# Filling the idle half of the PE array: two chunks of F of the last step, made beside the last turns of the second row tile

## The chip, the cores and the metric

The kernel runs on one core of a Trainium2 chip. Its measure is the device time of one execution in microseconds (us). Before the change the median of 3 runs is 686.38 us (685.98 to 687.02). The profile is one more execution of the same program, 683.8 us from its first to its last instruction. PE is the matrix engine (TensorE), PEld its weight loads, DVE the vector engine, ACT the scalar engine, POOL GpSimd and SP the queue that issues most transfers.

A matmul of this program holds one operand (the stationary one) in a part of the 128 x 128 array of PE and lets the columns of the other (the moving one) stream through. The part is a tile of rows x columns, written `64*64` in the profile: rows are the partitions that the sum runs over, columns are the partitions of PSUM that receive the result. "Row tile 0" means partitions 0 to 63 of the operands, "row tile 1" partitions 64 to 127. The two can work at once.

## The reference

```python
def _attn_ref(x, weight):            # x: 8 x 4096 x 192, weight: 8 heads x 7 taps
    w = softmax(weight, axis=-1)     # (shortened)
    x_pad = zeros of 6 rows in front of each sequence, then x
    out[b, s, h, :] = sum over k of w[h, k] * x_pad[b, s + k, h, :]

def _moe_ref(x, w_in, w_out, beta):  # x: 32768 x 192, F = 2048
    h = x @ w_in
    g = h * (1.0 / (1.0 + np.exp(-beta * h)))
    return (g @ w_out).astype(np.float32)
```

A causal convolution of seven taps runs over each sequence, and its result goes through a two-layer network with F = 2048 hidden values. The second product, `g @ w_out`, is what the change touches: 2048 values of F are 16 chunks (`fc`) of 128, one chunk to a matmul.

## The kernel before

The 32768 tokens are two streams (`s` = 0 and 1) of 16384, and the program goes over both in 36 steps, most of them 512 tokens of each stream. In a step `mm1` makes `ph` from the convolved tokens, ACT makes `g` of it (128 partitions of F x 2 streams x 512 tokens for each of 16 chunks), and the second product of the step before is made beside it by `mm2_quarters`. There the first 64 partitions of a chunk go to row tile 0 and the last 64 to row tile 1, the two streams to the two column halves, and the 192 outputs are done in thirds (`A`, `B_`, `C`). Row tile 1 follows row tile 0 at a distance of `LAG` = 8 turns, so that the two never write one bank of PSUM at once; so after the loop 8 turns are left in which only row tile 1 has work.

```python
    A, B_, C = range(NM)
    LAG = 8
    turns = [[], [None] * LAG]
    for i in range(NQ, n_steps - 1):
        for r, thirds in enumerate(((A, B_, C), (C, A, B_))):
            turns[r] += [(i, m, fc) for m in thirds for fc in range(NF)]
    turns[0] += [None] * LAG
    turns = list(zip(*turns))

    def mm2_quarters(count):
        for _ in range(count):
            turn = turns.pop(0)
            for s in range(NS):
                for r in range(2):
                    if turn[r] is None:
                        continue
                    i, m, fc = turn[r]
                    # ... (the bank po_of[i, m] is taken at the first turn)
                    pin(nc.tensor.matmul(po_of[i, m][half_of(s), 0:n], w_out_s[half_of(r), fc, m:D:NM],
                                         g_at(i, fc)[half_of(r), s, 0:n], ...))
            # ... (a third that is complete goes out: take_third, a transpose on DVE)
```

The last step has no later step to be hidden beside. `last` first makes the 8 turns that are left, and then the second product of the last step, with matmuls over the whole array: for each stream four blocks of 128 tokens, for each block 16 chunks.

```python
    def last(i):
        t0, n = steps[i]
        mm2_quarters(len(turns))
        for s in range(NS):
            for b in range(n // 128):
                po = po_bank()
                for fc in range(NF):
                    pin(nc.tensor.matmul(po[:, 0:D], g_at(i, fc)[:, s, ts(b, 128)], w_out_s[:, fc, :],
                                         start=(fc == 0), stop=(fc == NF - 1)))
                o_sb = osb_pool.tile([128, 2, D], FP32, name="o_sp", bufs=4)
                take_out(o_sb[:, 0, :], po)
                pin(nc.sync.dma_start(out=os_[s, t0 + 128 * b:t0 + 128 * (b + 1), :], in_=o_sb[:, 0, :]))
```

The loop over the steps, shortened to what matters here:

```python
        for u in range(0, NF, du):
            mm1(i, us)                       # 12 matmuls 64*64, and ACT's silu after them
            # ...
            if i > NQ:
                mm2_quarters(NM)             # 3 turns
            vector_work(i, ...)              # the convolution of later steps, on DVE
    assert not work
    last(n_steps - 1)
```

[...]`psum_h` holds two tiles `ph` of two banks each, `psum_o` four banks `po`.

Of the kernel before, what the change touches and what calls it, by code (L numbers as in the profile page):

```python
# [10 lines left out]
FP32 = mybir.dt.float32  # L11
FP32R = mybir.dt.float32r
BF16 = mybir.dt.bfloat16
# [6 lines left out]
def kernel(  # L20
# [9 lines left out]
    nc = tc.nc  # L30

    B, S, D = x.shape
# [4 lines left out]
    NF = F // 128  # L37
    NK = 3
    Q = D // NK
    NS = 2  # L40
    TS = B * S // NS
    TILE = 512
# [3 lines left out]
    def pin(ins):  # L46

        return tc.keep_in_program_order(ins)
# [4 lines left out]
    consts = ctx.enter_context(tc.tile_pool(name="consts", bufs=1))  # L53
# [7 lines left out]
    psum_h = ctx.enter_context(tc.tile_pool(name="psum_h", bufs=2, space=bass.MemoryType.PSUM))  # L61
# [10 lines left out]
    n_steps = len(steps)  # L72
# [33 lines left out]
    w_out_s = consts.tile([128, NF, D], BF16, name="w_out_s")  # L106
    w_out_v = moe_w_out.rearrange("(c p) d -> p c d", p=128)

    def half_of(s):
        return slice(64 * s, 64 * s + 64)  # L110
# [59 lines left out]
    def po_bank():  # L170
        return psum_o.tile([128, TILE], FP32, name="po")
# [146 lines left out]
    def mm1_pair(i, u):  # L318

        n = steps[i][1]  # L320
        ph = psum_h.tile([128, NS, TILE], FP32, name="ph")
        fcs = (u, u + NF // 2)
        for kk in range(NK):
            for h in range(2):
                pin(nc.tensor.matmul(ph[:, h, 0:NS * n], w_in_s[half_of(h), kk, ts(fcs[h], 128)],  # L325
                                     xc_of[i][half_of(h), :, kk, :],
                                     start=(kk == 0), stop=(kk == NK - 1)))
        for h in range(2):
            pin(nc.scalar.activation(g_at(i, fcs[h])[:, :, 0:n],  # L329
                                     ph[:, h, 0:NS * n].rearrange("p (s t) -> p s t", s=NS), AF.Silu,  # L330
                                     scale=beta[:, fcs[h]:fcs[h] + 1]))
# [19 lines left out]
    def g_at(i, fc):  # L351
        return g_of[i, fc // (NF // 2)][:, fc % (NF // 2), :, :]
# [4 lines left out]
    def mm2_plan(i):  # L357


        prs = pairs_of(i)  # L360
        order = [(prs[p], ph, 8 * ph + 4 * p, 8 * ph + 4 * p + 4) for ph in range(2) for p in range(2)]
        plan = [[] for _ in range(NF)]
        for pr, ph, u0, u1 in order:
            for n in range(NF):
                plan[u0 + n * (u1 - u0) // NF].append((pr, ph, n))
        return plan

    def mm2(i, pr, phase, fc):
        if phase == 0 and fc == 0:
            po_of[i, pr] = po_banks()  # L370
        po = po_of[i, pr]
        for half in range(2):
            q = half ^ phase
            s, b = pr[q]
            r = half_of(half)
            pin(nc.tensor.matmul(po[q][:, 0:D], g_at(i, fc)[r, s, ts(b, 128)], w_out_s[r, fc, :],  # L376
                                 start=(phase == 0 and fc == 0), stop=(phase == 1 and fc == NF - 1)))
        if phase == 1 and fc == NF - 1:
            store(i, pr, po)

    def take_out(dst, po):
        pin(nc.vector.tensor_copy(dst, po[:, 0:D]))  # L382
# [20 lines left out]
    turns = [[], [None] * LAG]  # L403
# [3 lines left out]
    turns[0] += [None] * LAG  # L407
    turns = list(zip(*turns))

    def mm2_quarters(count):  # L410
        for _ in range(count):
            turn = turns.pop(0)
            for s in range(NS):
                for r in range(2):
# [3 lines that stand above are left out]
                    if (i, m) not in po_of:  # L418
                        po_of[i, m] = po_bank()
                    first = r == (m == C)  # L420
                    n = steps[i][1]
                    pin(nc.tensor.matmul(po_of[i, m][half_of(s), 0:n], w_out_s[half_of(r), fc, m:D:NM],  # L422
                                         g_at(i, fc)[half_of(r), s, 0:n],
                                         start=(first and fc == 0), stop=(not first and fc == NF - 1)))
            for r in range(2):
                if turn[r] is not None:
                    i, m, fc = turn[r]
                    if fc == NF - 1 and r != (m == C):
                        take_third(i, m)
# [4 lines left out]
    def take_third(i, m):  # L434
        nonlocal budget
        n = steps[i][1]
        if i not in osb_of:
            osb_of[i] = osb_pool.tile([128, TILE // L, L, NM], FP32, name="o_sb", bufs=2)
        pin(nc.vector.transpose(osb_of[i][:, 0:n // L, :, m],  # L439
                                po_of[i, m][:, 0:n].rearrange("p (b l) -> p b l", l=L)))  # L440
        budget -= (n + 60) / 0.96
        if m != B_:
            return
        t0, n = steps[i]
        for s in range(NS):
            dst = os_[s, t0:t0 + n, :].rearrange("(b l) (g d) -> g l b d", l=L, g=2)
            for g in range(2):
                p = 64 * s + L * g
                pin(nc.sync.dma_start(out=dst[g],
                                      in_=osb_of[i][p:p + L, 0:n // L, :, :].rearrange("p b l m -> p b (l m)")))  # L450

    def last(i):

        t0, n = steps[i]
        mm2_quarters(len(turns))
        for s in range(NS):
            for b in range(n // 128):
                po = po_bank()
                for fc in range(NF):
                    pin(nc.tensor.matmul(po[:, 0:D], g_at(i, fc)[:, s, ts(b, 128)], w_out_s[:, fc, :],  # L460
                                         start=(fc == 0), stop=(fc == NF - 1)))
                o_sb = osb_pool.tile([128, 2, D], FP32, name="o_sp", bufs=4)
                take_out(o_sb[:, 0, :], po)
                pin(nc.sync.dma_start(out=os_[s, t0 + 128 * b:t0 + 128 * (b + 1), :], in_=o_sb[:, 0, :]))
# [21 lines left out]
    def vector_work(i, ns, flush=False):  # L486


        nonlocal budget
        budget += ns  # L490
        while work and ((budget > 0 and work[0][0] <= i + 2) or (flush and work[0][0] <= i + 1)):
            budget -= work[0][1]
            work.pop(0)[2]()
        budget = min(budget, 0.0) if work else 0.0

    def new_g(i, half):
        n, kind = (TILE, "g") if i > 1 else (128, "gp")
        g_of[i, half] = g_pool.tile([128, NF // 2, NS, n], BF16, name=f"{kind}{half}")
# [58 lines left out]
    for i in range(n_steps):  # L557
        plan = mm2_plan(i - 1) if NP <= i <= NQ else [[] for _ in range(NF)]
        new_g(i, 0)
        if i < NP:  # L560
            new_g(i, 1)
        if i < NP:
            for u in range(NF // 2):
                mm1_pair(i, u)
                first_tile(i, u)
                for ph in (0, 1):
                    for j in range(i):
                        for fc in first_mm2.get((i, u, j, ph), ()):
                            mm2(j, prs_0, ph, fc)
                if i == 2:  # L570
                    vector_work(i, 1300, flush=u == NF // 2 - 1)
            continue
        du = 2 if steps[i][1] == 256 else 1
        for u in range(0, NF, du):
            us = range(u, u + du)
            if u == NF // 2:
                new_g(i, 1)
            mm1(i, us)
            for v in us:
                for t in plan[v]:  # L580
                    mm2(i - 1, *t)
                    if t[1] == 1 and t[2] == NF - 1:
                        budget -= 2 * (D + 60) / 0.96
            if i > NQ:
                mm2_quarters(NM)
            vector_work(i, 1307 * du * steps[i][1] // TILE, flush=u + du == NF)
    assert not work
    last(n_steps - 1)
# [1 line left out]
_INS = ['x', 'weight', 'moe_w_in', 'moe_w_out', 'moe_beta']  # L590
# [26 lines left out]
```

## Time and profile before

| | before |
|---|---|
| time, median of 3 runs | 686.38 us (685.98 to 687.02) |
| span of the profiled execution | 683.8 us |
| PE busy | 679.2 us, 99% |
| ACT busy | 584.0 us, 85% |
| DVE busy | 551.1 us, 81% |
| first product, line 343 | 5952 matmuls |
| second product beside it, line 422 | 5568 matmuls |
| second product of the last step, line 460 | 128 matmuls |
| granted PE clock | 1.000 |

Line numbers are those of the kernel file. A row of the timeline gives the start of the first instruction (us from the start of the span), how long the run of like instructions lasted, engine, line, operation, output and inputs, the shape, and how many were merged; in square brackets how long the engine had been idle before and what ended that. The ends of matmuls are modelled by the profiler, so their starts are the thing to read: the duration of a 64*64 matmul over 512 columns is given as 0.38 us, although the next one on the same part of the array starts earlier than that. The last microseconds, from about 667 us on, are where the change acts.

### The profile page before, as it was taken

What the parts mean: (1) busy time and instruction counts of PE and PEld (TensorE: products, weight loads), DVE (VectorE), ACT (ScalarE), POOL (GpSimd) and SP (SyncE); (2) the same over time, 40 slices, a digit from 0 to 9 for tenths busy, and PEclk for the clock granted to TensorE, in tenths of its full rate; (3) what the DMA queues carried; (4) which work ended last, traced back from release to release, by engine and by line L of the source; (5) the groups of instructions that cost most, each with busy time, mean ns of one, the idle gap of its engine ahead of it and who ended that gap; (6) DMA issues with size and microseconds to landing.
All of it is one profiled execution on the core that took longest, in us unless ns stands there. A gap on an engine that the chain in (4) does not pass through costs nothing.

```text
span 683.8 us, 27210 instructions
## 1 busy us (share of the span) xinstructions
PE 679.2 (99%) x12528; PEld 460.5 (67%) x12528; DVE 551.1 (81%) x886; ACT 584.0 (85%) x585; POOL 14.5 (2%) x26
## 2 busy tenths in 40 slices
PE   9999999999999999999999999999999999999998
PEld 7799887666666666666666666666666666666667
DVE  5999999999988888878889888889888889875112
ACT  7999999888888888888888888888888888888881
POOL 8000000000000000000000000000000000000000
PEclk9999999999999999999999999999999999999999
DMA  9652534244432344423344423344324343320223
GB/s 207 183 134 85 146 95 122 75 117 118 117 78 66 106 106 117 117 61 80 103 112 117 111 57 88 103 115 117 99 46 108 103 118 71 68 49 6 49 48 94
DMA packets 150418, 66.85 MB, mean 98 GB/s; under 512 B 113648, under 2 KB 149696, under 8 KB 150304
## 3 DMA queue, kind: packets, MB, share of 16 engines
q1 hardware_dynamic: 146992, 61.08, 35.0%
q0 software_dynamic: 3168, 3.93, 2.7%
q8 instruction: 98, 1.61, 1.0%
q14 instruction: 16, 0.13, 0.1%
q10 hardware_dynamic: 144, 0.10, 0.1%
HBM read 28.32 MB, written 25.17 MB: 78 GB/s over the span
## 4 chain that ended last, share of the span: by engine, by line
PE 98%; POOL 1%; DMA 1%; ACT 0%; issue 0%; DVE 0%; POOLq 0%
PE ph L343 47%; PE po L422 43%; PE po L376 4%; PE po L460 2%; PE ph L325 1%; DMA w_in_s<-in_moe_w_in_dram 1%; POOL w_in_s L113 0%; PE po L229 0%; ACT gp L329 0%; POOL xb L131 0%; PE po L215 0%; POOL sel L146 0%; DVE o_sp L382 0%; POOL ident L148 0%; POOLq L146 0%
## 5 line engine op out<-in xcount | busy, mean ns | idle before, releaser
L348 ACT ACTIVATE g<-ph,beta 128x1024 bf16<-128x1024 f32 (+2 forms) x528 | 557.3, 1063 | 80.9 <-PE ph L343 61.8
L343 PE MATMUL ph<-xc,w_in_s 64*64 64x512 bf16 (+3 forms) x5952 | 613.1, 368 | 0.0
L422 PE MATMUL po<-g,w_out_s 64*64 64x512 bf16 (+1 forms) x5568 | 580.7, 372 | 0.0
L343 PEld LDWEIGHTS <-w_in_s 64*64 64x64 bf16 (+1 forms) x5952 | 275.3, 104 | 125.3 <-issue 0.4
L422 PEld LDWEIGHTS <-w_out_s 64*64 64x64 bf16 x5568 | 290.3, 118 | 83.9
L303 DVE SCALAR_TENSOR_TENSOR acc<-xt,tapn,acc 128x512 f32<-128x512 bf16 (+2 forms) x450 | 311.1, 758 | 0.9
L439 DVE STREAM_TRANSPOSE o_sb<-po 128x512 f32<-128x512 f32 (+1 forms) x87 | 76.5, 879 | 111.5 <-PE po L422 111.5
L303 DVE SCALAR_TENSOR_TENSOR xc<-xt,tapn,acc 128x512 bf16<-128x512 bf16 (+2 forms) x90 | 63.9, 759 | 0.2
L87 DVE CAST xb<-xf 128x768 bf16<-128x768 f32 (+1 forms) x62 | 49.0, 830 | 0.2 <-DMA xf<-in_x_dram 0.2
L301 DVE TENSOR_SCALAR acc<-xt,tapn 128x512 f32<-128x512 bf16 (+2 forms) x90 | 41.0, 486 | 1.1
L376 PE MATMUL po<-w_out_s,g 64*128 64x192 bf16 x512 | 28.3, 243 | 0.0
L376 PEld LDWEIGHTS <-g 64*128 64x128 bf16 x512 | 23.5, 94 | 1.6
L382 DVE COPY o_sp<-po 128x192 f32<-128x192 f32 x28 | 9.0, 353 | 8.2 <-PE po L460 7.3
L325 PE MATMUL ph<-xcp,w_in_s 64*128 64x256 bf16 (+1 forms) x144 | 15.1, 306 | 0.5 <-DMA w_in_s<-in_moe_w_in_dram 0.2
L329 ACT ACTIVATE gp<-ph,beta 128x256 bf16<-128x256 f32 x32 | 12.7, 477 | 1.3 <-PE ph L325 1.0
L460 PEld LDWEIGHTS <-g 128*128 128x128 bf16 x128 | 10.5, 98 | 0.4 <-issue 0.4
L460 PE MATMUL po<-w_out_s,g 128*128 128x192 bf16 x128 | 10.7, 246 | 0.0
L329 ACT ACTIVATE g<-ph,beta 128x512 bf16<-128x512 f32 x16 | 9.6, 693 | 0.1
L325 PEld LDWEIGHTS <-w_in_s 64*128 64x128 bf16 x144 | 6.8, 94 | 4.1 <-issue 1.3
L376 PE MATMUL po<-w_out_s,gp 64*128 64x192 bf16 x128 | 7.6, 243 | 0.0
L376 PEld LDWEIGHTS <-gp 64*128 64x128 bf16 x128 | 6.0, 94 | 1.6
L229 PE MATMUL po<-xr,diag 64*128 64x384 f32 x49 | 7.0, 361 | 0.0
(52 smaller groups left out, 57.0 us busy)
## 6 DMA issues: line engine op xcount, KB each, us to landing
xf<-in_x_dram SPq DMA_DIRECT2D x60, 384.0 KB, 4.2
out_dram<-o_sb SPq DMA_DIRECT2D x108, 192.0 KB, 4.6
xt<-xb SPq DMA_TRANSPOSE x122, 3.1
out_dram<-o_sp SPq DMA_DIRECT2D x10, 192.0 KB, 4.0
w_out_f<-in_moe_w_out_dram POOLq DMA_DIRECT2D x4, 384.0 KB, 6.3
out_dram<-o_sb SPq DMA_DIRECT2D x8, 144.0 KB, 3.9
w_in_s<-w_in_s POOLq DMA_DIRECT2D x4, 192.0 KB, 7.4
out_dram<-o_sp SPq DMA_DIRECT2D x8, 96.0 KB, 1.8
```

The source lines that it names most:

```text
L87: pin((eng or nc.vector).tensor_copy(xbf_of[j][:, b0:b1, :, s, :].rearrange("p b k q -> p k b q"), xf_of[j][:, b0:b1, s, :].rearrange("p b ...
L301: pin(nc.vector.tensor_scalar_mul(a, src, w))
L303: pin(nc.vector.scalar_tensor_tensor(out=xc_of[i][:, k0:k1, o:o + m] if k == K - 1 else a, in0=src, scalar=w, in1=a, op0=ALU.mult, op1=ALU ...
L325: pin(nc.tensor.matmul(ph[:, h, 0:NS * n], w_in_s[half_of(h), kk, ts(fcs[h], 128)], xc_of[i][half_of(h), :, kk, :], start=(kk == 0), stop= ...
L329: pin(nc.scalar.activation(g_at(i, fcs[h])[:, :, 0:n], ph[:, h, 0:NS * n].rearrange("p (s t) -> p s t", s=NS), AF.Silu, scale=beta[:, fcs[ ...
L343: pin(nc.tensor.matmul(ph[m0:m1, s, n * e:n * e + n], w_in_s[half_of(s), kk, 128 * fc + m0:128 * fc + m1], xc_of[i][half_of(s), kk, 0:n], ...
L348: pin(nc.scalar.activation(g_at(i, fc)[:, :, 0:n], ph[:, :, n * e:n * e + n], AF.Silu, scale=beta[:, fc:fc + 1]))
L376: pin(nc.tensor.matmul(po[q][:, 0:D], g_at(i, fc)[r, s, ts(b, 128)], w_out_s[r, fc, :], start=(phase == 0 and fc == 0), stop=(phase == 1 a ...
L382: pin(nc.vector.tensor_copy(dst, po[:, 0:D]))
L422: pin(nc.tensor.matmul(po_of[i, m][half_of(s), 0:n], w_out_s[half_of(r), fc, m:D:NM], g_at(i, fc)[half_of(r), s, 0:n], start=(first and fc ...
L439: pin(nc.vector.transpose(osb_of[i][:, 0:n // L, :, m], po_of[i, m][:, 0:n].rearrange("p (b l) -> p b l", l=L)))
L460: pin(nc.tensor.matmul(po[:, 0:D], g_at(i, fc)[:, s, ts(b, 128)], w_out_s[:, fc, :], start=(fc == 0), stop=(fc == NF - 1)))
```

## The change

Beside the 8 turns in which row tile 0 has nothing to do, it is to make two chunks (`NX` = 2) of F for the four blocks of stream 0 of the last step. Row tile 0 sees only partitions 0 to 63. The lower half of a chunk lies there already; the upper half of `g` and of `w_out_s` is copied there by DVE in the last step (`copy_low`), into `g_x` and `w_x`. So each of four blocks gets four matmuls of 64 rows instead of two of 128 rows: 16 matmuls `64*128` over 192 columns, two to a turn. Four banks must be open at once for that; two are `po` banks and two come from one more `ph` tile. Afterwards the four blocks of stream 0 have only chunks 2 to 15 left.

```diff
-    def mm2_quarters(count):
-        for _ in range(count):
+    def mm2_quarters(count, beside=()):
+
+        per = -(-len(beside) // count)
+        for n_turn in range(count):
             turn = turns.pop(0)
             for s in range(NS):
                 for r in range(2):
 ... (the matmuls of the turn)
+            for mm in beside[per * n_turn:per * n_turn + per]:
+                mm()
             for r in range(2):
                 if turn[r] is not None:
                     i, m, fc = turn[r]
 ...
+    NX = 2
+    g_x = consts.tile([64, NX, TILE], BF16, name="g_x")
+    w_x = consts.tile([64, NX, D], BF16, name="w_x")
+
+    def copy_low(i):
+        pin(nc.vector.tensor_copy(w_x, w_out_s[half_of(1), 0:NX, :]))
+        for fc in range(NX):
+            pin(nc.vector.tensor_copy(g_x[:, fc, :], g_at(i, fc)[half_of(1), 0, :]))
+
     def last(i):
 
         t0, n = steps[i]
-        mm2_quarters(len(turns))
+        ph = psum_h.tile([128, NS, TILE], FP32, name="ph")
+        banks = [po_bank(), ph[:, 0, :], ph[:, 1, :], po_bank()]
+        r0 = half_of(0)
+        beside = []
+        for b in range(n // 128):
+            for fc in range(NX):
+                for g, w in ((g_at(i, fc)[r0, 0, :], w_out_s[r0, fc, :]), (g_x[:, fc, :], w_x[:, fc, :])):
+                    beside.append(lambda b=b, g=g, w=w, start=len(beside) % (2 * NX) == 0: pin(
+                        nc.tensor.matmul(banks[b][:, 0:D], g[:, ts(b, 128)], w, start=start, stop=False)))
+        mm2_quarters(len(turns), beside)
         for s in range(NS):
             for b in range(n // 128):
-                po = po_bank()
-                for fc in range(NF):
+                po = po_bank() if s else banks[b]
+                f0 = 0 if s else NX
+                for fc in range(f0, NF):
                     pin(nc.tensor.matmul(po[:, 0:D], g_at(i, fc)[:, s, ts(b, 128)], w_out_s[:, fc, :],
                                          start=(fc == 0), stop=(fc == NF - 1)))
 ...
             vector_work(i, 1307 * du * steps[i][1] // TILE, flush=u + du == NF)
+            if (i, u) == (n_steps - 1, NX + 1):
+                copy_low(i)
```

## The prediction

> **What bounds the kernel now.** I read the page first: its row of busy times and the chain that ended last.
>
> ```profile
> PE 679.2 (99%) x12528; PEld 460.5 (67%) x12528; DVE 551.1 (81%) x886; ACT 584.0 (85%) x585; POOL 14.5 (2%) x26
> ...
> PE 98%; POOL 1%; DMA 1%; ACT 0%; issue 0%; DVE 0%; POOLq 0%
> ```
>
> PE is busy throughout and carries 98% of the chain. So whatever takes time off PE's sequence at the end takes it off the total, and whatever adds to it adds to the total. DVE and ACT have slack. The change touches nothing before the last step, so I then took the timeline of the last microseconds, PE alone:
>
> ```profile
> 667.05 0.38 PE L343 MATMUL ph<-xc,w_in_s 64*64 64x512 bf16 x2
> 667.23 0.38 PE L422 MATMUL po<-g,w_out_s 64*64 64x512 bf16 x2
> 667.27 0.38 PE L343 MATMUL ph<-xc,w_in_s 64*64 64x512 bf16 x2
> 667.45 0.38 PE L422 MATMUL po<-g,w_out_s 64*64 64x512 bf16 x2
> 667.48 0.38 PE L343 MATMUL ph<-xc,w_in_s 64*64 64x512 bf16 x2
> 667.66 2.11 PE L422 MATMUL po<-g,w_out_s 64*64 64x512 bf16 x24
> 669.71 0.42 PE L460 MATMUL po<-w_out_s,g 128*128 128x192 bf16 x3
> ```
>
> Two things are to be seen. One line's pairs repeat every 0.216 us (667.05, 667.27, 667.48): that is a turn of 512 columns. And pairs of line 422 start between those of line 343, 0.03 us ahead of them, although the program puts all of line 343 of an `mm1` first: the two row tiles are at different places of the program, and row tile 1 is ahead. The sixth row says by how much. From 667.66 its 24 matmuls start over 2.11 - 0.38 = 1.73 us, that is 8 steps of 0.216, so 9 turns. Were row tile 0 working in all of them there would be 36; 24 is 3 turns with 4 matmuls and 6 with 2. The program has 8 turns with row tile 1 alone, so two of them were already done beside row tile 0's last work. What row tile 0 has free is about 6 x 0.216 = 1.30 us less the 0.03 us, 1.26 us.
>
> The same stretch on the vector engine:
>
> ```profile
> 668.56 0.89 DVE L439 STREAM_TRANSPOSE o_sb<-po 128x512 f32<-128x512 f32 x1 [2.12 <-PE po L422]
> 669.81 0.87 DVE L439 STREAM_TRANSPOSE o_sb<-po 128x512 f32<-128x512 f32 x1 [0.36 <-PE po L422]
> 671.24 0.36 DVE L382 COPY o_sp<-po 128x192 f32<-128x192 f32 x1 [0.56 <-PE po L460]
> 672.56 0.36 DVE L382 COPY o_sp<-po 128x192 f32<-128x192 f32 x1 [0.96 <-PE po L460]
> 673.88 0.36 DVE L382 COPY o_sp<-po 128x192 f32<-128x192 f32 x1 [0.96 <-PE po L460]
> ```
>
> The transposes at 668.56 and 669.81 are the last thirds of row tile 0 and of row tile 1, 1.25 us apart, which agrees with 1.26. A block of 16 full-array matmuls is ready every 1.32 us, so one costs 82.5 ns.
>
> Last I looked at every place where PE goes from one tile shape to another, with narrow windows of the timeline. The first two rows are the end of the 64*64 work, the next two the one place where 64*128 gives way to 64*64 (the step in which `mm1` changes its shape), the last two a change from 128*128 to 64*128.
>
> ```profile
> 669.17 0.60 PE L422 MATMUL po<-g,w_out_s 64*64 64x512 bf16 x4
> 669.70 0.20 PEld L460 LDWEIGHTS <-g 128*128 128x128 bf16 x3 [0.40 <-issue]
> ...
> 74.70 0.49 PE L376 MATMUL po<-w_out_s,g 64*128 64x192 bf16 x7
> 75.12 0.14 PEld L343 LDWEIGHTS <-w_in_s 64*64 64x64 bf16 x8 [0.16 <-issue]
> ...
> 19.53 0.39 PE L215 MATMUL po<-ident_b,xb 128*128 128x128 bf16 x4
> 19.84 0.10 PEld L376 LDWEIGHTS <-gp 64*128 64x128 bf16 x2
> ```
>
> The last start of a row is its start plus its length less one duration. First pair: 669.17 + 0.60 - 0.376 = 669.39; the next matmul starts at 669.71 with its weight load: 0.31 us instead of 0.216, so 0.09 lost. Second: 74.70 + 0.49 - 0.243 = 74.95, next at 75.12: 0.17 instead of 0.0825, again 0.09. Third: 19.53 + 0.39 - 0.219 = 19.70, next at 19.84: 0.145 instead of 0.057, 0.09. So three changes of shape cost 90 ns each, whatever the shapes, and the next weight load never starts earlier, while inside one shape it is hidden.
>
> [...]
>
> **The change part by part.**
>
> Removed: two of 16 chunks for four blocks, 8 full-array matmuls x 82.5 ns = 0.66 us off PE's sequence.
>
> Added on DVE: three copies over 64 partitions, two of 512 and one of 384 elements. A copy of 128 x 384 elements out of PSUM took 0.36 us (the copy at 19.78 us of the timeline), so about 1.2 us at most as an estimate from it. DVE sat idle for 13.14 us before the transpose at 665.55 us, and the copies are issued early in the last step, over 10 us ahead of their use. Cost 0.
>
> The banks: the new `ph` tile must wait for the silu of the last `mm1` but one. ACT ran that from 666.63 to 667.74 us; the first use of the tile is in the third of the eight turns, later than that. The `po` banks belonged to thirds that were taken out long before. Cost 0.
>
> Added on PE: 16 matmuls 64*128 over 192 columns. Were they only work on an idle row tile, 16 x 82.5 ns = 1.32 us against the 1.26 us that are free: hidden but for 0.06 us. But the program puts two of them behind the 64*64 pair of each turn. Each turn so changes the mode twice, and a mode change stops both row tiles, not only the one that changes. That also ends row tile 1's lead. Step by step, with the starts of before:
> - Turn 1 of the eight: its pair can still run ahead (667.88, one turn after the 667.66 of before). The first added matmul must wait for row tile 0's last one to end: that starts in the third turn of that row, at 668.13 with the 0.03 us, plus 0.216 plus 0.09 = 668.44.
> - Its two matmuls: 94 ns for the first (after the change at 669.71 the second matmul starts 94 ns later, because the load is not hidden) and 82.5 for the second, then 0.09 for the change back: the pair of turn 2 starts at 668.71.
> - Each further turn: pair 0.216, plus about 0.025 for its load (after 75.12 the next turn of 384 columns comes 0.187 us later instead of 0.162), plus 0.09, plus 0.094, plus 0.0825, plus 0.09: 0.60 us instead of 0.216.
> - The pair of turn 8 starts at 668.71 + 6 x 0.60 = 672.31, its first added matmul at 672.64, the second at 672.74, and the first full-array matmul at 672.74 + 0.0825 + 0.09 = 672.91, where before it started at 669.71: 3.20 us later.
>
> Sum: +3.20 - 0.66 = +2.54 us, and 686.38 + 2.54 = 688.9 us. Nothing behind it changes: blocks come every 1.16 us in stream 0 and every 1.32 in stream 1, DVE needs 0.36 for each, and the last copy and its transfer (3.3 us from 680.48 to 683.8) stay as they are.
>
> **The rivals.**
> - The added matmuls are hidden, as meant: two shapes on different row tiles run at once. Then -0.66 + 0.06 = -0.60 us, 685.8 us. For it: the row tiles do run apart from each other. Against it: row tile 1 never ran on across a change of shape in this trace, and the kernel itself gives `mm1` 64*128 in the steps whose second product is 64*128, and 64*64 only where that is 64*64.
> - Only one direction of the change drains, or the drain is shorter where the streaming work is short: about half of 3.2, +1.0 us, 687.4 us. Against it: 90 ns in all three, both narrower to wider and wider to narrower.
> - In order, without drain, but not at once: 16 x 82.5 ns more, 0.66 fewer, and the lead of two turns lost (0.4): +1.1 us, 687.5 us. Hard to tell from the one before by the time alone; the starts tell them apart.
> - A wait for a bank or for the copies takes part in it: the numbers above leave no room for one; it would add to any of these.
>
> **Range and chances.** I give the drain 0.82, the two middle cases together 0.08, the hidden case 0.10. In the drain case the spread comes from the runs (685.98 to 687.02) and from 15 changes whose cost could be 70 to 110 ns (0.3 us either way): 688.0 to 689.8. The range of 8 in 10, 687.2 to 690.1, takes in that and the top of the middle cases. 2% is 13.7 us, more than four times any of these, so within 2% is nearly certain.
>
> **What would show it right or wrong.** In the changed profile the timeline after 667.7 should show pairs of line 422 and pairs of the added line by turns, 0.60 us from pair to pair, each weight load after a gap put down to issue, and the first matmul of line 460 near 672.9. The transposes of the last two thirds should be 4 us apart instead of 1.25. If 422 keeps its 0.216 us with the added matmuls between, the drain is wrong and the time is 685.8. If the pairs come 0.38 us apart, there is no drain, only order. If PE waits for DVE or ACT there, my bank and copy steps are wrong.

## The result and the profile after

The changed kernel takes 691.3 us, median of 4 runs (690.29 to 692.62), against 686.64 us before (685.98 to 687.02, 4 runs): a ratio of 1.0071 with an interval of 1.0056 to 1.0086. It is 4.7 us slower, within 2%, and above the range of the prediction.

First the two lines of the page that were read before: busy times, and the shares of the chain that ended last.

```profile
PE 683.5 (99%) x12536; PEld 461.8 (67%) x12536; DVE 551.5 (80%) x889; ACT 583.4 (85%) x585; POOL 14.6 (2%) x26
...
PE 97%; DMA 1%; POOL 1%; ACT 0%; issue 0%; DVE 0%; POOLq 0%
```

They hide what happened. PE is "busy" 99% as before, since a matmul's modelled end covers a pause of 0.1 us after it (a 64*64 matmul of line 424 is given 0.38 us, where a turn inside one shape is 0.216). Only the eight more matmuls (16 added, 8 removed) and three more instructions on DVE are seen. The story is in the timeline of the changed kernel. Line 424 is the turns (422 before), 479 the added matmuls, 486 the blocks of the last step (460 before). The first row is the first 64*64 matmul of the program and will serve as a common zero.

```profile
75.78 0.52 PE L343 MATMUL ph<-xc,w_in_s 64*64 64x384 bf16 x8
...
668.32 0.85 PE L424 MATMUL po<-g,w_out_s 64*64 64x512 bf16 x10
...
669.10 0.09 PEld L479 LDWEIGHTS <-g 64*128 64x128 bf16 x1 [0.40 <-issue]
669.10 0.25 PE L479 MATMUL po<-w_out_s,g 64*128 64x192 bf16 x1
...
669.20 0.24 PE L479 MATMUL po<-w_x,g_x 64*128 64x192 bf16 x1
...
669.37 0.12 PEld L424 LDWEIGHTS <-w_out_s 64*64 64x64 bf16 x2 [0.16 <-issue]
669.37 0.42 PE L424 MATMUL po<-g,w_out_s 64*64 64x512 bf16 x2
669.72 0.09 PEld L479 LDWEIGHTS <-g 64*128 64x128 bf16 x1 [0.23 <-issue]
...
669.99 0.42 PE L424 MATMUL po<-g,w_out_s 64*64 64x512 bf16 x2
...
673.72 2.42 PE L486 MATMUL po<-w_out_s,g 128*128 128x192 bf16 x14
...
675.93 1.84 PE L486 MATMUL ph<-w_out_s,g 128*128 128x192 bf16 x14
...
677.82 0.36 DVE L382 COPY o_sp<-ph 128x192 f32<-128x192 f32 x1 [1.28 <-PE ph L486]
678.23 1.32 PE L486 MATMUL ph<-w_out_s,g 128*128 128x192 bf16 x14 [0.45 <-DVE o_sp L382]
...
679.38 6.60 PE L486 MATMUL po<-w_out_s,g 128*128 128x192 bf16 x78
...
686.01 0.36 DVE L382 COPY o_sp<-po 128x192 f32<-128x192 f32 x1 [0.96 <-PE po L486]
```

Three things are to be seen.

1. The shapes alternate and nothing runs at once. A pair of line 424 at 669.37, the next at 669.99: 0.617 us a turn (669.37 to 673.07 for six turns), where before the change it was 0.216. Each weight load after a change of shape starts late, after 0.16 to 0.40 us of idle time, and its wait is put down to issue.
2. The first block of the last step, 14 matmuls from 673.72, takes until 675.93: 2.21 us where 14 x 82.5 ns = 1.16. The second block is stretched too: it starts its last matmul at 675.93 + 1.84 - 0.25 = 677.52, after 1.59 us where 13 x 82.5 ns = 1.07 is due. Blocks after that run at the old speed, 1.15 us for 14 matmuls (678.23 to 679.38).
3. The third block, at 678.23, waited for a copy on DVE, that of the second block (677.82 to 678.18). Its predecessor's last matmul began at 677.52, so 0.71 us lie between them instead of 0.08.

The second is the clock. In the view of stretches each row gives the stretch, its length, the busy time and count of PE, PEld, DVE, ACT and POOL, then the granted clock, the DMA share and GB/s:

```profile
669.10:673.70 4.60, 4.60 (x32) 1.74 (x30) 1.03 (x2) 0.59 (x1) 0.00 (x0) 0.99 0.00 0
673.70:677.00 3.30, 3.30 (x22) 3.10 (x22) 1.06 (x2) 0.00 (x0) 0.00 (x0) 0.50 0.45 105
677.00:680.00 3.00, 2.55 (x31) 2.41 (x30) 0.71 (x2) 0.00 (x0) 0.00 (x0) 1.00 0.81 212
```

At the end of the alternation PE gets half its clock, for 3.4 us: narrower windows show 0.50 from 673.60 to 677.00. A full-array matmul costs 160 ns there (2.21 us for 14).

The program's start varies from one execution to another: the first 64*64 matmul came at 75.12 us before and at 75.78 here, and at 76.64 in another trace of the same changed kernel. So the traces are compared from that matmul on. From the kernel before:

```profile
75.12 0.52 PE L343 MATMUL ph<-xc,w_in_s 64*64 64x384 bf16 x8
...
680.48 0.36 DVE L382 COPY o_sp<-po 128x192 f32<-128x192 f32 x1 [0.96 <-PE po L460]
```

Before: first full-array matmul at 669.71 - 75.12 = 594.59, last copy at 680.48 - 75.12 = 605.36. After: 673.72 - 75.78 = 597.94 and 686.01 - 75.78 = 610.23. The loss on this scale is 4.87 us, and it adds up:

| part | us |
|---|---|
| alternation: first full-array matmul later | +3.35 |
| 8 full-array matmuls fewer | -0.66 |
| slowed clock: (2.21 - 1.16) + (1.59 - 1.07) | +1.57 |
| third block waits for DVE: 0.71 - 0.08 | +0.63 |
| sum | +4.89 |

### The profile page after: what moved, and what is told of

Same layout as the page of the kernel before. It is cut to its first block, busy times and chain, and to the rows that moved or that the text cites. A ratio compares the mean times of both kernels' runs of the same rounds, so it can differ in the third digit from the quotient of the medians.

```text
span 689.4 us, 27229 instructions
## 1 busy us (share of the span) xinstructions
PE 683.5 (99%) x12536; PEld 461.8 (67%) x12536; DVE 551.5 (80%) x889; ACT 583.4 (85%) x585; POOL 14.6 (2%) x26
## 4 chain that ended last, share of the span: by engine, by line
PE 97%; DMA 1%; POOL 1%; ACT 0%; issue 0%; DVE 0%; POOLq 0%
PE ph L343 47%; PE po L424 43%; PE po L376 4%; PE ph L325 1%; PE po L486 1%; DMA w_in_s<-in_moe_w_in_dram 1%; POOL w_in_s L113 0%; PE ph L486 0%; PE po L229 0%; ACT gp L329 0%; POOL xb L131 0%; PE po L479 0%; PE ph L479 0%; DVE o_sp L382 0%; PE po L215 0%
## 5 line engine op out<-in xcount | busy, mean ns | idle before, releaser
L486 PE MATMUL po<-w_out_s,g 128*128 128x192 bf16 x92 | 9.0, 264 | 0.0
```

## The experiments

The theory: (a) each change of shape stops PE on both row tiles, so the order of the matmuls is what costs; (b) the wait before the third block comes from two banks being halves of one tile; (c) the slowed clock answers to the pauses. The rivals: the added matmuls themselves can't run beside the others; DVE is simply late; the clock answers to half of the array being idle. Ten runs took them apart. Each was timed beside the kernel before the change, on the same chip.

**The same shape.** The added work as 64*64 matmuls, one for each half of 64 tokens:

```diff
+                    for c in range(2):
+                        beside.append(... nc.tensor.matmul(banks[b][half_of(c), 0:D],
+                                          g[:, ds(128 * b + 64 * c, 64)], w, ...))
-                    beside.append(... nc.tensor.matmul(banks[b][:, 0:D], g[:, ts(b, 128)], w, ...))
```

> The added matmuls in the same tile shape as the turns: 32 of 64*64 in two column halves instead of 16 of 64*128, all else as in the changed kernel. If the change of shape is what costs, a turn of the second row tile stays at 0.216 us, the added work lies beside it, and the granted clock stays at 1.000: 8 x 82.5 ns = 0.66 us saved, less 0.06 us that does not fit, plus the 0.61 us for which PE waits for DVE before the third block: 686.6 us, the same as before the change within 0.3. If the added matmuls themselves can't run beside the others, each turn grows by at least 0.165 us: 687.9 us or more.

Measured: 686.28 us (13 runs) against 686.24, ratio 1.0005 (0.9997 to 1.0013). Its timeline on PE, line 480 being the added matmuls:

```profile
667.50 0.85 PE L424 MATMUL po<-g,w_out_s 64*64 64x512 bf16 x12
668.19 0.25 PE L480 MATMUL po<-w_out_s,g 64*64 64x192 bf16 x2
...
668.46 0.38 PE L424 MATMUL po<-g,w_out_s 64*64 64x512 bf16 x2
668.52 0.25 PE L480 MATMUL ph<-w_out_s,g 64*64 64x192 bf16 x2
668.60 0.25 PE L480 MATMUL ph<-w_x,g_x 64*64 64x192 bf16 x2
668.67 0.38 PE L424 MATMUL po<-g,w_out_s 64*64 64x512 bf16 x2
...
669.63 1.33 PE L488 MATMUL po<-w_out_s,g 128*128 128x192 bf16 x14
...
672.56 1.32 PE L488 MATMUL ph<-w_out_s,g 128*128 128x192 bf16 x14 [0.45 <-DVE o_sp L382]
```

The turns keep their 0.216 us (668.46 to 668.67) with two or three pairs of the added matmuls between, 0.08 us each. With its first 64*64 matmul at 74.96 the first full-array matmul comes at 594.67, 0.08 us later than before the change: the work is hidden. The rival that it can't run beside the others falls. The wait for DVE is still there and eats the gain.

**Two tiles.** The changed kernel's shapes, with the borrowed banks apart:

```diff
-        ph = psum_h.tile([128, NS, TILE], FP32, name="ph")
-        banks = [po_bank(), ph[:, 0, :], ph[:, 1, :], po_bank()]
+        ph, ph2 = [psum_h.tile([128, NS, TILE], FP32, name="ph") for _ in range(2)]
+        banks = [po_bank(), ph[:, 0, :], po_bank(), ph2[:, 0, :]]
```

> The changed kernel with its two borrowed banks in two tiles ph instead of one, the shapes left as they are. If PE's wait of 0.61 us before the third block is there because the second block's bank is in the same tile and is still being read by DVE, it goes away and the time falls by 0.6 us to about 690.7; the alternation of shapes at 0.617 us a turn and the slowed clock after it stay. If the wait is for DVE being late with anything else, it stays and the time is 691.3.

Measured: 691.18 us (5 runs) against 686.24, ratio 1.0070 (1.0058 to 1.0083). The time alone shows nothing of the 0.6 us: five runs spread over 1.6 us. The timeline on PE does:

```profile
674.36 2.42 PE L486 MATMUL po<-w_out_s,g 128*128 128x192 bf16 x14
676.57 1.90 PE L486 MATMUL ph<-w_out_s,g 128*128 128x192 bf16 x14
678.31 1.32 PE L486 MATMUL po<-w_out_s,g 128*128 128x192 bf16 x14
679.46 1.32 PE L486 MATMUL ph<-w_out_s,g 128*128 128x192 bf16 x14
```

The third block follows the second without a wait, and unhindered blocks are 1.15 us apart. From its first 64*64 matmul (76.45) to the last copy (686.10) it takes 609.65 us, 0.58 less than the changed kernel, with about as much slowed clock (the first two blocks take 2.21 and 1.74 us; in the changed kernel 2.21 and, without the wait, 1.67). The copy on DVE follows the second block's last matmul by 0.3 us in both traces (677.82 after 677.52, 678.51 after 678.22); DVE was not late, and what went away is that PE had to wait for it. The edit also moves the third block from a `ph` bank to a `po` bank, but a `ph` bank as such does not bring the wait: the fourth block has one here and starts at 679.46, ahead of the copy of the third at 679.66. The clock was below 0.999 in all five runs.

**Both.**

> Both edits together. If shapes and tile are the whole cause: 0.66 us saved less 0.06 us, no wait, no slowed clock: 686.0 us, 0.6 us under the kernel before the change. If the added matmuls cost by themselves: 687.3 us.

Measured: 685.67 us (21 runs) against 686.24, ratio 0.9990 (0.9984 to 0.9997). On PE:

```profile
669.56 1.33 PE L488 MATMUL po<-w_out_s,g 128*128 128x192 bf16 x14
670.72 1.32 PE L488 MATMUL ph<-w_out_s,g 128*128 128x192 bf16 x14
671.88 1.32 PE L488 MATMUL po<-w_out_s,g 128*128 128x192 bf16 x14
673.03 1.32 PE L488 MATMUL ph<-w_out_s,g 128*128 128x192 bf16 x14
```

Four short blocks without a gap. From the first 64*64 matmul (74.89) to the last copy (679.67) it takes 604.78 us, 0.58 less than before the change. This version does what the change was for. It is faster than the kernel before by a thousandth, and 5.6 us under the 691.3 us of the changed one.

**The changes of shape with next to no work.** The added matmuls take 32 columns and go to a bank that nothing reads; the blocks make all 16 chunks.

```diff
+                        nc.tensor.matmul(ph[:, 0, 0:32], g[:, ts(b, 128)], w[:, 0:32], start=True, stop=True)
-                        nc.tensor.matmul(banks[b][:, 0:D], g[:, ts(b, 128)], w, start=start, stop=False)
```

> The 16 changes of shape with next to no work in them: the added matmuls take 32 columns instead of 192 and go to a bank that nothing reads, and the last step's blocks make all 16 chunks again. If the changes of shape cost, a turn is about 0.48 us instead of 0.216 and the first full-array matmul comes 2.3 us later than before: 688.9 us with the clock at 1.000, and up to 1.5 us more if the slowed clock comes with it. If only the amount of added work costs, it is 16 x 16 ns = 0.3 us at most: 686.9 us.

Measured: 689.29 us (5 runs, 688.04 to 690.06) against 686.24, ratio 1.0040 (1.0028 to 1.0053). On PE:

```profile
672.01 0.42 PE L424 MATMUL po<-g,w_out_s 64*64 64x512 bf16 x2
672.37 0.19 PE L478 MATMUL ph<-w_out_s,g 64*128 64x32 bf16 x1
672.40 0.17 PE L478 MATMUL ph<-w_x,g_x 64*128 64x32 bf16 x1
672.51 0.42 PE L424 MATMUL po<-g,w_out_s 64*64 64x512 bf16 x2
...
673.49 2.73 PE L484 MATMUL po<-w_out_s,g 128*128 128x192 bf16 x31
```

A turn takes 0.49 us. Its work is 0.216 and, as an estimate by columns, twice 32 / 192 of 80 ns, 0.03; the other 0.25 us are two changes of shape. With the first 64*64 matmul at 76.58 the first full-array one comes at 596.91, 2.32 us later than before the change. So 2.32 of the 3.35 us are there with next to no work. The missing 1.03 us are about what the 160 columns left out of each added matmul would take by the same estimate: 16 x 0.0825 x 160 / 192 = 1.10.

**Half the changes, the same work.** Four added matmuls behind every second turn:

```diff
-            for mm in beside[per * n_turn:per * n_turn + per]:
+            for mm in beside[per * (n_turn - 1):per * (n_turn + 1)] if n_turn % 2 else ():
```

> The changed kernel with its 16 added matmuls in four groups of four, one behind every second turn: 8 changes of shape instead of 16, the same work. If each change costs its 0.13 us, two turns take about 0.98 us instead of 2 x 0.617, so the first full-array matmul comes 1.0 us earlier: 688.5 us at a clock of 1.000, and up to 1.6 us more if the slowed clock stays. If the cost is that of the added work, not of its order, the time stays at 691.3 us.

Measured: 688.48 us (12 runs) against 686.54, ratio 1.0028 (1.0019 to 1.0037). On PE, two turns and the group behind them:

```profile
670.84 0.64 PE L424 MATMUL po<-g,w_out_s 64*64 64x512 bf16 x4
671.41 0.25 PE L479 MATMUL ph<-w_out_s,g 64*128 64x192 bf16 x1
...
671.84 0.64 PE L424 MATMUL po<-g,w_out_s 64*64 64x512 bf16 x4
```

1.00 us for two turns; less 2 x 0.216 and 4 x 0.0825 that leaves 0.24 us for two changes. The changed kernel gives (0.617 - 0.216 - 0.165) / 2 = 0.12 us for one as well, and the kernel with next to no work 0.125. The same figure from three kernels: each change of shape costs 0.12 us, with two matmuls of 192 or 32 columns between, or with four of 192. The added work costs its own time on top, 16 x 0.0825 = 1.32 us, since it is not hidden. The clock stayed at 0.999 or above in all 12 runs.

**All behind.** The added matmuls after the eight turns, with two tiles:

```diff
-        mm2_quarters(len(turns), beside)
+        mm2_quarters(len(turns))
+        for mm in beside:
+            mm()
```

> The added matmuls all behind the eight turns, with the two borrowed banks in two tiles: one change of shape more than before the change, but nothing runs beside them. 0.09 us for the change and 1.33 us for 16 matmuls one after the other, less 0.66 us: 687.0 us, clock 1.000[...]. If the slowed clock answers to the shape 64*128 or to the added matmuls, it shows here too and the time is 688.6 us.

Measured: 687.18 us (13 runs) against 686.54, ratio 1.0010 (1.0002 to 1.0018). Row tile 1's lead is back, with 24 matmuls in one row as before the change, and one change of shape follows:

```profile
668.22 2.11 PE L424 MATMUL po<-g,w_out_s 64*64 64x512 bf16 x24
670.27 0.25 PE L479 MATMUL po<-w_out_s,g 64*128 64x192 bf16 x1
670.36 0.24 PE L479 MATMUL po<-w_x,g_x 64*128 64x192 bf16 x1
...
671.69 1.33 PE L488 MATMUL po<-w_out_s,g 128*128 128x192 bf16 x14
```

The first full-array matmul comes 1.42 us after that of before (671.69 - 75.68 = 596.01), as expected, at full clock. So shape 64*128 as such brings no slowed clock (0.999 or above in all 13 runs), and not even giving up the overlap costs as much as overlapping with the wrong shape (+1.42 us to that matmul against +3.35).

**The changed kernel again.**

> The changed kernel once more, beside the others: 691.3 us. The granted clock is below 1.000 in most executions, each with a stretch near the end of the program in which a full-array matmul takes 160 ns instead of 82.5.

Measured: 692.39 us (4 runs) against 686.54, ratio 1.0080 (1.0066 to 1.0094), with a granted clock of 0.994 to 0.998 in all four. Its trace takes 610.20 us from the first 64*64 matmul (76.64) to the last copy (686.84), the same as the first time. With the four runs above that is 7 of 8 with a slowed clock. The run without had 690.29 us, the shortest of the eight.

**Half of the array, no pauses.** The kernel before with 32 more turns of row tile 1 alone (added work):

```diff
+        for t in range(32):
+            for s in range(NS):
+                pin(nc.tensor.matmul(ph[half_of(s), 0, 0:n], w_out_s[half_of(1), t % 8, B_:D:NM],
+                                     g_at(i, t % 8)[half_of(1), s, 0:n], start=True, stop=True))
```

> The kernel before the change with 32 more turns in which only the second row tile works, in one shape and without gaps, into a bank that nothing reads (added work, the output is whole): 32 x 0.216 = 6.91 us more. If the slowed clock comes from the pauses of the alternation, it stays away: 693.2 us at 1.000. If it comes from half of the array lying idle[...], it comes here for sure, since the stretch is 8 us long: 1.6 us or more on top, 694.8 us, clock 0.998 or lower.

Measured: 693.68 us (4 runs) against 686.54, ratio 1.0099 (1.0085 to 1.0113); the clock was 1.000 in all four. In the view of stretches the 8 us with only row tile 1:

```profile
669.90:678.00 8.10, 8.10 (x77) 4.57 (x74) 1.77 (x2) 0.48 (x1) 0.00 (x0) 1.00 0.40 97
```

The rival for the clock falls: half of the array lying idle doesn't slow it by itself, even for 8.1 us instead of 4.6. Whether pauses slow it when the other half works too stays open: in every alternating pattern here row tile 0 or row tile 1 was idle as well.

**Longer stretches.** Two kernels followed by 8 further turns of their own pattern into a bank that nothing reads:

> The kernel with 8 changes of shape, followed by 8 further turns of the same pattern into a bank that nothing reads (added work, the output is whole): its stretch of alternation is 7.8 us instead of 3.9, with four groups more at 0.98 us per two turns, so 3.9 us more: 692.4 us. If the clock slows whenever the alternation lasts longer than about 4 us, it is below 1.000 in most executions here and 1.6 us or more come on top: 694 us. If it slows only where the pauses take a large share of the time (38% of it in the changed kernel, 22% here), it stays at 1.000.

Measured: 692.71 us (6 runs) against 686.88, ratio 1.0102 (1.0078 to 1.0127). The clock was 1.000 in four runs, 0.993 and 0.995 in two.

> The kernel whose added matmuls have 32 columns, followed by 8 further turns of the same pattern into a bank that nothing reads: a stretch of alternation of 7.9 us instead of 3.9, with pauses for about half of it; 8 x 0.492 = 3.9 us more: 693.2 us. Both by length and by the share of the pauses the clock should now be below 1.000 in nearly all executions, where the short one had it in 1 of 5, and 1.6 us or more come on top: 695 us. If it stays at 1.000, neither is the cause and the columns of the added matmuls matter.

Measured: 696.17 us (4 runs) against 686.88, ratio 1.0142 (1.0129 to 1.0155). The clock was 0.992 to 0.995 in all four, and in the trace it is halved while the alternation still lasts and beyond:

```profile
674.00:678.00 4.00, 4.00 (x22) 1.29 (x20) 0.20 (x1) 0.00 (x0) 0.00 (x0) 0.50 0.67 162
678.00:682.00 4.00, 4.00 (x27) 3.17 (x26) 0.24 (x1) 0.00 (x0) 0.00 (x0) 0.50 0.14 35
682.00:686.00 4.00, 4.00 (x39) 3.83 (x37) 0.84 (x3) 0.00 (x0) 0.00 (x0) 0.74 0.16 52
```

Together, for the clock (pauses: what a turn's matmuls don't fill, as a share of the turn; stretch: from the first added matmul to the first full-array one in the traces, for half of the array without pauses the 8 us above; in the last row the slowed clock has itself stretched it, at full clock it would be 3.6 + 8 x 0.492 = 7.5 us):

| pattern | pauses | stretch | runs with a clock below 0.999 |
|---|---|---|---|
| one shape, half of the array | 0 | 8.1 us | 0 of 4 |
| 8 changes | 24% | 3.4 us | 0 of 12 |
| 8 changes, longer | 24% | 7.4 us | 2 of 6 |
| the changed kernel, and with two tiles | 38% | 4.6 us | 12 of 13 |
| 16 changes, little work | 51% | 3.6 us | 1 of 5 |
| the same, longer | 51% | 9.2 us | 4 of 4 |

By these few runs both the share of the pauses and the length of the stretch count: neither alone orders the rows, and where the line runs stays open. The four traces with a slowed clock narrow the length down. In them it fell 4.1 to 4.6 us after the first added matmul (669.10 to 673.60 in the changed kernel, 669.78 to 673.83 in the last row, worked out from narrow windows). So in the last row it was not the whole length that was needed: the clock fell 0.5 us after the point where the shorter pattern of the row above ends. That the pauses are the cause rests on the comparison with the first row; a slowed clock also turned up once in the 13 runs of the same-shape kernel (0.997), so it isn't wholly confined to alternation.

## Why the prediction missed

Its central step held. Every change of shape stopped both row tiles, and the overlap never came about: +3.35 us to the first full-array matmul where 3.20 was predicted (a turn 0.617 us instead of 0.60; the entry into 64*128 takes 0.35 us from the start of a pair, not 0.33). When I predicted, only the 0.09 us at three changes was measured, and that both row tiles stop was my assumption. The changed kernel shows it: line 424, on row tile 1 alone, takes 0.617 us a turn where it took 0.216, with nothing but line 479 on row tile 0 between. The prediction's "mode" is the tile shape, and its "drain" this stop; whether PE was empty at each, as that word says, was not shown, since the ends of matmuls are modelled in the trace; the starts show the stop. The saving of 0.66 us, the copies at no cost, and the loss of row tile 1's lead came out as worked out. The prediction from these alone would have been 2.7 us instead of 2.54. Two steps failed, and the 1.57 and 0.63 us that they left out are what the range lacked:

- "Nothing behind it changes: blocks come every 1.16 us in stream 0" failed. The first two blocks took 2.21 and 1.67 us, because the clock was halved for 3.4 us. This is the term that was missing from the sum, not one of the wrong size. I had taken the clock of before, 1.000, as given, and asked only what the pauses cost while they last, not what they trigger. The trace of before could not answer that: its granted clock is 1.000, and from 20 us on it has two changes of shape in all (75.12 and 669.71), while in the pattern that I predicted myself pauses fill more than a third of a turn. The trace of the changed kernel shows 0.50 for 3.4 us, after turns of 0.617 us with two pauses of about 0.12 us each, and nowhere in the alternation were two starts more than 0.36 us apart: many short pauses went ahead of the fall, not a long one. By what rule the clock falls was not shown.
- "Cost 0" for the banks, and of a wait for a bank "the numbers above leave no room for one", failed. I checked when the new tile could first be written, but not its later life: blocks two and three have their banks in one tile, and PE's first write of the third block waited until DVE had copied out the second, although that is another bank. The two-tile kernel settles it: without the shared tile the wait of 0.63 us is gone.

That a load is hidden inside one shape holds on the same rows as well. In the last step of the kernel before, matmul and load both use 128 rows, and the loads lie beside the matmuls, one every 82.5 ns:

```profile
669.70 10.51 PEld L460 LDWEIGHTS <-g 128*128 128x128 bf16 x128 [0.40 <-issue]
669.71 10.73 PE L460 MATMUL po<-w_out_s,g 128*128 128x192 bf16 x128
```

Of the rivals, the hidden case is what the same shape with two tiles gives (0.6 us saved, measured 0.57 on the medians and 0.58 in the trace). For the changed kernel it was rightly given little weight. The sign was right, and the size was short by 4.66 - 2.54 = 2.1 us, about the sum of the two missing terms, 2.2 us.

## What to carry to other kernels

Fill an idle part of the PE array only with matmuls of the tile shape that runs beside it: here a change of shape cost about 0.12 us and stopped both row tiles, and sixteen of them (1.9 us) cost more than the work they were to hide (1.32 us). When a change puts pauses between PE's instructions, ask what the granted clock will do after them, and leave room for it in the range: here it was 0.50 for 3.4 us, which cost 1.57 us. And give each bank of PSUM that is read on its own a tile of its own: here the read of one half held up the writes to the other for 0.63 us.

## What was not expected of the hardware

Row tile 1 started matmuls two turns ahead of row tile 0 in the kernel before, in one instruction stream; the changes of shape among the turns took that lead away (10 matmuls in the row of line 424 at 668.32 instead of 24), and putting the added work behind the turns gave it back (24 at 668.22). Two 64*64 matmuls in the two column halves over 192 columns cost 0.08 us together with their weight loads beside a busy row tile, the same as one over the whole array. And pauses of about 0.12 us at a time went ahead of a fall of the clock to half (0.50), 4.1 to 4.6 us after the first added matmul in the traces; on the whole it was below 0.999 in 12 of 13 executions of one pattern, while 8 us with half of the array and no pauses left it at 1.000.
